# q turned by VectorE instead of TensorE, and v loaded by two heads, from the third batch on, in a threshold attention with a SoLU feed-forward layer

## The chip, the cores and the metric

The kernel runs on one core of a Trainium2 chip. The metric is the device time of one execution in microseconds; each kernel is run several times and the median is given. A profile is of one execution, and its span, from the first to the last instruction, is slightly shorter than the device time of that execution.

## The reference

Inputs are float32: q, k and v of 8 batches, 8 heads, 576 rows and 64 columns, and the weights of a feed-forward layer (w_in and w_out arrive as float64, 512 KB for 128x512). Cut to what matters:

```python
scores = scale * np.matmul(q, k.transpose(0, 1, 3, 2))          # scale = 1/8
thresh = np.max(scores, axis=-1, keepdims=True) - tau
scores = np.where(scores >= thresh, scores, -1000000000.0)
attn = softmax(scores)
x = np.matmul(attn, v)           # then (B,H,S,D) -> (B*S, H*D): 4608 x 512
h = x @ w_in                     # 4608 x 1024
solu = h * softmax(h)
ln = (solu - mean) / sqrt(var + 1e-06) * g_ln
out = ln @ w_out                 # 4608 x 512
```

The softmax is over all 576 keys of a row; the order in which keys are summed and queries are computed is free, as long as q's rows, k's rows, v's rows and the output's rows are matched.

## The kernel before

**Tiling.** Heads are taken in pairs: pair i holds heads 2hp and 2hp+1 of batch b, with i = 4b + hp, so there are 32 pairs. A pair's q and k are needed with the 64 columns of each head on the partitions (`qT`, `kT`: 128 partitions, two heads). The 576 queries of a pair are worked on as two kinds of 256 queries each (kind 0 and 1) and a rest of 64 (kind 2, which takes the rests of all four pairs of a batch together, from `qe`). A slot is 128 queries of two heads against 576 keys; a batch has 18 slots (PER), the program has 144 (NS).

**Rounds.** The program is one hand-written order of all engines' instructions (`tc.manual_schedule`): a loop over rounds `rnd`, one slot of scores each, in which every engine gets its share. In a round TensorE computes the scores of the slot (L460, into the PSUM tiles s0 and s1, which have one buffer each), then a quarter of the feed-forward work: half of the first product (`ff_h`, L625) or half of the second (`ff_o`, L729), so that two h rounds and two o rounds follow one another. In h rounds it also does one product with v (`attend_steps`, L569), due three or more rounds after the slot. VectorE takes the row maxima (`maxes`, L482), ScalarE the ramp and the exponential (`ramp` L497, `exps` L506), GpSimd the normalising in the next round (L513 to L516), VectorE then transposes the weights in 32x32 blocks (`blocks`, L528), and three or four DMAs move them into `wT` (L537 to L544). The feed-forward steps (L640 to L717) are spread over the rounds by the lists `middle` and `late`, and `ff_out` and `ff_store` copy and store the output.

**q and k.** For batches 0 and 1, TensorE transposes q and k with an identity (`turn`, L324) into spare columns of s0 and s1, ahead of the scores of a round, and ScalarE and VectorE copy the results out (`q_item`: L360 and L364; `e_item` for the last 64 rows: L404 and L408; `k_item`: L385). The list `preps` says in which round an item may go. From batch 2 on, k is treated in another way: `load_natural` loads it with four DMAs of 32 partitions per pair, in an order of keys (i, a, t) with 9 keys in a run, `turn_natural` transposes it on VectorE in 32x32 blocks (L192) into `flip`, and two DMAs write it to `kT` (L195). q still goes through `preps`: four turns and one for the rest, for each pair. The dictionaries `load_at` and `turn_at` give the rounds.

**v.** For b > 1, `load_v` loads four heads into a tile of 128 partitions: both halves of the partitions hold all four heads, since the weights of two groups of queries lie on the two halves. It uses four DMAs, each of two heads to 64 partitions.

**Queues.** All loads, moves and stores in the steady part are issued by SP, in program order. A DMA that waits for an engine holds up those behind it. In a round SP gets, in this order: the swap of V (L707), the moves to wT, the stores (L756), the writes of a turned k (L195), then the loads.

**Buffers.** The tiles q, k and ends have two buffers, v three, qT six, kT and qe seven, flip one. They decide from which round on a load can start.

Of the kernel before, what the change touches and what calls it, by code (L numbers as in the profile page):

```python
# [8 lines left out]
F32 = mybir.dt.float32  # L9
# [11 lines left out]
def kernel(  # L21
# [128 lines left out]
    def load_v(b, hf, parts=(0, 1, 2)):  # L150
        d = halves.setdefault((b, hf), {})
        hs = slice(4 * hf, 4 * hf + 4)

        if b > 1:
            if 0 in parts:
                d["v"] = loads.tile([P, 4, NK, D], F32, tag="v", bufs=3, name="v")
            for part in parts:
                two, u = divmod(part, 2)
                nc.sync.dma_start(
                    out=d["v"][ROWS[u], 2 * two : 2 * two + 2].rearrange("p h m d -> p h (m d)"),  # L160
                    in_=v[b, hs][2 * two : 2 * two + 2].rearrange("h (p m) d -> p h (m d)", m=NK),
                )
            return
        if 0 in parts:
            d["v"] = loads.tile([P, 4, NK, D], F32, tag="v", bufs=3, name="v")
        rest = v[b, hs, 0:SM, :].rearrange("h (p t) d -> p h (t d)", t=4)
        for part, to, rows, of in (
            (0, 0, slice(0, P), slice(0, P)), (1, 4, ROWS[0], ROWS[1]), (1, 4, ROWS[1], ROWS[0])
        ):
            if part in parts:  # L170
                nc.sync.dma_start(
                    out=d["v"][rows, :, to : to + 4].rearrange("p h t d -> p h (t d)"),
                    in_=rest[of],
                )
        for rows in ROWS if 2 in parts else ():
            nc.sync.dma_start(
                out=d["v"][rows, :, NK - 1], in_=v[b, hs, SM:S, :].rearrange("h p d -> p h d")
            )

    def load_natural(i):  # L180
        b, hp = divmod(i, NP)
        src = k[b, 2 * hp : 2 * hp + 2].rearrange("h (i a t) d -> a h i (t d)", a=2, t=NK)
        raw = loads.tile([P, 4, 4, D], F32, tag="k", name="k")
        natural[i] = raw = raw.rearrange("p h t d -> p (h t d)")[:, 0 : NK * D]
        for g in range(4):
            a, h = divmod(g, 2)
            nc.sync.dma_start(out=raw[32 * g : 32 * g + 32], in_=src[a, h])

    def turn_natural(i):
        raw = natural.pop(i)  # L190
        flip = loads.tile([P, 2, NK, 32], F32, tag="flip", bufs=1, name="flip")
        nc.vector.transpose(out=flip, in_=raw.rearrange("p (t x g) -> p g t x", g=2, x=32))  # L192
        to = pair(i)["kT"]
        for a in range(2):
            nc.sync.dma_start(  # L195
                out=to[:, 32 * NK * a : 32 * NK * (a + 1)],
                in_=flip[ROWS[a]].rearrange("p g t x -> p g (t x)"),
            )
# [119 lines left out]
    def turn(spare, x, lhsT_of, rows=2, swap=False):  # L318

        o = spare["base"] + 64 * x  # L320
        to = slice(o, o + 64)
        for r in range(rows):
            for y in range(2):
                nc.tensor.matmul(  # L324
                    out=spare[r][ROWS[y], to], lhsT=lhsT_of(r, y),
                    rhs=swapped[ROWS[1]] if swap and r else ident[ROWS[r], ROWS[r]],
                    start=True, stop=True,
                )
# [9 lines left out]
    def pair(i):  # L338
        if i not in pairs:
            pairs[i] = dict(  # L340
                qT=heads.tile([P, SM], F32, tag="qT", bufs=6, name="qT"),
                kT=heads.tile([P, S], F32, tag="kT", name="kT"),
                qe=heads.tile([P, ST], F32, tag="qe", name="qe"),
            )
        return pairs[i]
# [46 lines left out]
    def e_item(i):  # L392
        src, h0 = source(i)
        last = k_parts(i)[:, NK - 1] if i < 2 * NP else None

        def make(spare, x):
            turn(
                spare, x, lambda r, y: ends[i // NP][ROWS[r], 2 * (i % NP) + y],
                2 if i < 2 * NP else 1,
            )  # L400

        def keep(spare, x, r):
# [4 lines left out]
            elif last is not None:  # L407
                (nc.scalar.copy if spare.get("eased") else nc.vector.tensor_copy)(  # L408
                    out=last, in_=seen(spare, 1, x, 1)[:, 0].rearrange("p (k c) -> p c k", c=2)
                )  # L410
# [28 lines left out]
    def scores(s, items):  # L439
# [10 lines left out]
        for ks in (slice(SM, S), slice(0, SM)):  # L450
            for h in range(2):
                for y in range(2):
                    if kind < 2:
                        d = pairs[b * NP + hp]
                        t = P * (2 * kind + r) + 64 * y
# [92 lines left out]
    def attend_steps(key):  # L548
# [7 lines left out]
        for e in range(2) if kind == 2 else [None]:  # L556
            for m in range(NK):
                for u in range(2):
                    d, h0 = source(b * NP + (hp if e is None else e + 2 * u))
                    for h in range(2):  # L560
                        if e is None:
                            to = y[ROWS[h], u, 0:P].rearrange("p (r g x) -> p g r x", r=2, g=2)
                            rhs = wT[ROWS[u], :, m, :, h]
                        else:
# [5 lines left out]
                            out=to, lhsT=d["v"][ROWS[u], h0 + h, m ^ 4 * u if m < 8 and b < 2 else m],  # L570
# [5 lines left out]
    def attended(key):  # L576
        b, kind, hp = key
        tag, y = units.pop(key)["y"]
        y = y.rearrange("p (u n) -> p u n", u=2)[:, :, 0:P].rearrange("p u (r y) -> p u r y", r=2)
# [6 lines left out]
        else:  # L586
# [4 lines left out]
            to = xh[b, kind][:, hp].rearrange("p (r u y) -> p u r y", r=2, u=2)  # L591
# [130 lines left out]
    def ff_o(t, part):  # L722
        d = ffn[t]
        if part == 0:
            d["otag"], d["o"] = take("o_ps")
        for m in range(NC * part, NC * part + NC):
            for r in range(2):
                for z in range(2):
                    nc.tensor.matmul(  # L729
                        out=d["o"][ROWS[z], 512 * r : 512 * r + 256],  # L730
# [16 lines left out]
    def ff_store(t, last):  # L747
        d = ffn.pop(t)
        if len(t) == 1:
            rows = out.rearrange("(b s) m -> s b m", s=S)[SM:S, 2 * t[0] : 2 * t[0] + 2]  # L750
# [25 lines left out]
    for i in range(NP, NPAIR):  # L776
        b, hp = divmod(i, NP)
        if b == 1:
            at = (13, 15, 19, 20)[hp]
        else:  # L780
            at = PER * (b - 1) + ((6, 12, 16, 21) if b == 2 else (6, 9, 12, 17))[hp]
        if b == 1:
            preps += [
                (at, 3, lambda i=i: k_item(i, slice(0, 3)), i),
                (at, 1, lambda i=i: k_item(i, slice(3, 4)), i),
            ]
        preps += [
            (at, 1, lambda i=i: e_item(i), i),
# [4 lines left out]
    turn_at = {}  # L793
# [11 lines left out]
    for i in range(2 * NP, NPAIR):  # L805
        b, hp = divmod(i, NP)
        if b == 2:
            at = (24, 30, 34, 39)[hp]
        else:
            at = PER * b + 4 * hp - (11 if b % 2 else 13)  # L810
        turn_at[at] = i
        load_at.setdefault(at - 3, []).append(lambda i=i: load_natural(i))
        if hp % 2:
            load_at.setdefault(PER * (b - 1) + (9 if hp == 3 else -1), []).append(
                lambda b=b, hf=hp // 2: load_one(b, hf, "q")
            )
            at, by = (PER * b + 4, 1) if hp == 3 else (PER * b - 9, 2)
            for part in range(4):
                load_at.setdefault(at + by * part, []).append(
                    lambda b=b, hf=hp // 2, part=part: load_v(b, hf, (part,))  # L820
                )

    with tc.manual_schedule():
# [29 lines left out]
        while True:  # L853
# [88 lines left out]
            elif step == ("h", 1):  # L942
# [9 lines left out]
                late.setdefault(at, []).append(lambda t=cur, at=at: ff_turn(t, at))  # L952
# [27 lines left out]
            for job in late.pop(rnd, []):  # L980
                job()
            if rnd in turn_at:
                turn_natural(turn_at[rnd])
# [48 lines left out]
```

## Time and profile before

| | before |
|---|---|
| runs | 879.71 us median of 3 (874.94 to 881.91) |
| profiled execution | 880.11 us, span 878.3 us |
| mean granted TensorE clock | 0.979 (0.82 and 0.84 in the first 109 us, then 1.00) |
| L324, TensorE transposes | 1440 records, 35.23 us busy |
| L360, q copied by ScalarE | 480 ns for 128x256 |
| L364, q copied by VectorE | 479 ns for 128x256, 26 from s_ps |
| L404, rest of q copied by ScalarE | 313 ns for 128x64, 28 from s_ps |
| L192, k transposed by VectorE | 24 of 732 ns |
| L516, weights scaled by GpSimd | 288 of 770 ns |
| SP issues: k, 72 KB | 96, 4.1 us to landing |
| SP issues: q, 512 KB | 15, 5.1 us to landing |
| SP issues: v, 288 KB | 48, 4.8 us to landing |
| SP issues: kT from flip, 144 KB | 48, 2.6 us to landing |
| SP issues: wT, 288 KB | 160, 6.5 us to landing |
| DMA moved | 161.59 MB, the ring that SP uses busy 72.6% of 16 engines' span |

The page gives for each engine the time in which it was busy, its share of the span and the number of its instructions (PE is TensorE, PEld its weight loads, DVE VectorE, ACT ScalarE, POOL GpSimd). Under it stand rows of 40 digits: the busy share of each fortieth of the span, in tenths. A line in order of time has the start, the duration, the engine, the line of the code, the operation, what it writes and reads, how many were merged, and in brackets the idle time of the engine ahead of it with what ended it. A TensorE matmul of float32 leaves two records; the ends of matmuls are modelled, and records overlap in time since four 64x64 tiles of the array work at once.

### The profile page before, as it was taken

Reading aid. Unit: us, or ns where it says so; the run is one execution under the profiler, and the core shown is the slowest. Engines: PE = TensorE matmul, PEld = TensorE weight load, DVE = VectorE, ACT = ScalarE, POOL = GpSimd, SP = SyncE. Lnnn points to the kernel's source line nnn. Section 1 sums busy time; section 2 is a strip of 40 time slices with the busy share of each in tenths; the row PEclk is TensorE's granted clock in tenths of the full one; section 3 lists DMA queues with packets and bytes.
Section 4 is the critical chain, followed back from the end, with each engine's and each line's share of the span. In section 5 each row is a group of like instructions: output and inputs, shape, how many; then the busy total and the mean of one; then the engine's idle time right before and its main releaser. Section 6 shows DMA issues by size and latency. Waiting matters only on the chain. (4 is left out here: it accounts for less than half of the span.)

```text
span 878.3 us, 37901 instructions
## 1 busy us (share of the span) xinstructions
PE 831.3 (95%) x16225; PEld 585.2 (67%) x16225; DVE 680.0 (77%) x1248; ACT 586.8 (67%) x1201; POOL 471.0 (54%) x890
## 2 busy tenths in 40 slices
PE   4677899999999999999999999999999999999997
PEld 3353676866677777777776766777677677777655
DVE  5998787888788888888788888888778887877351
ACT  5977776777767777777667667777676776775121
POOL 2877655555555555555555555555455555555120
PEclk9878899999999999999999999999999999999999
DMA  7999877887877777887778786887678776765322
GB/s 231 276 255 256 203 189 190 209 220 175 197 190 205 193 184 186 214 201 168 175 179 215 185 200 169 196 218 185 159 182 221 179 178 152 177 140 139 66 49 49
DMA packets 84008, 161.59 MB, mean 184 GB/s; under 512 B 18808, under 2 KB 48512, under 8 KB 83840
## 3 DMA queue, kind: packets, MB, share of 16 engines
q1 hardware_dynamic: 82704, 157.17, 72.6%
q8 instruction: 127, 2.08, 1.1%
q10 hardware_dynamic: 1136, 2.00, 0.7%
q14 instruction: 41, 0.34, 0.1%
HBM read 46.14 MB, written 9.44 MB: 63 GB/s over the span
## 5 line engine op out<-in xcount | busy, mean ns | idle before, releaser
L482 DVE CUSTOM_DVE_ANT_0 w<-s_ps,tau_t 128x576 f32<-128x576 f32 x280 | 200.7, 754 | 123.4 <-PE s_ps L460 92.5
L497 ACT ACTIVATE w<-s_ps,nth 128x576 f32<-128x576 f32 x280 | 200.1, 743 | 107.5 <-DVE nth L482 101.3
L729 PE MATMUL o_ps<-w,uT 64*64 64x256 f32 x4608 | 264.5, 376 | 2.1 <-DVE uT L717 1.1
L729 PEld LDWEIGHTS o_ps<-w,uT 64*64 64x64 f32 x4608 | 218.8, 133 | 59.9 <-issue 16.8
L516 POOL TENSOR_SCALAR w<-w,sm 128x576 f32<-128x576 f32 x288 | 218.4, 770 | 14.3
L506 ACT ACTIVATE w<-w,ntau 128x576 f32<-128x576 f32 x288 | 220.2, 771 | 0.0
L625 PE MATMUL h_ps<-w,xh 64*64 64x512 f32 x1856 | 217.3, 592 | 0.0
L528 DVE STREAM_TRANSPOSE T<-w 128x576 f32<-128x576 f32 x288 | 206.2, 751 | 7.7 <-POOL w L516 7.4
L569 PEld LDWEIGHTS pv<-wT,v 64*64 64x64 f32 x5760 | 164.0, 136 | 50.5 <-issue 39.5
L460 PE MATMUL s_ps<-kT,qT 64*64 64x64 f32 (+1 forms) x2048 | 166.9, 423 | 16.6 <-ACT w L497 13.3
L569 PE MATMUL pv<-wT,v 64*64 64x128 f32 (+1 forms) x5760 | 167.5, 263 | 6.8 <-DMA wT<-T 3.5
L513 POOL TENSOR_SCALAR sm<-sm 128x2 f32<-128x2 f32 x144 | 36.5, 254 | 234.3 <-ACT w L506 231.2
L625 PEld LDWEIGHTS h_ps<-w,xh 64*64 64x64 f32 x1856 | 94.3, 134 | 98.4 <-issue 95.5
L514 POOL TENSOR_TENSOR sm<-sm,mone 128x2 f32<-128x2 f32 x144 | 104.3, 724 | 12.0
L691 ACT ACTIVATE V<-u,nb,rs 128x1024 f32<-128x1024 f32 x36 | 44.7, 1241 | 52.6 <-POOL nb L681 52.6
L460 PEld LDWEIGHTS s_ps<-kT,qT 64*64 64x64 f32 x2048 | 60.4, 139 | 24.8 <-ACT w L497 18.8
L592 ACT COPY xh<-pv 128x256 f32<-128x256 f32 x64 | 23.7, 370 | 61.4 <-PE pv L569 61.4
L506 ACT ACTIVATION_READ_ACCUMULATOR w<-w,ntau 128x1 f32 x288 | 56.7, 197 | 0.0
L696 DVE TENSOR_SCALAR u<-u,rs,nb 128x1024 f32<-128x1024 f32 x36 | 42.3, 1176 | 12.6 <-ACT V L691 12.4
L655 DVE TENSOR_TENSOR u<-h_ps,u 128x1024 f32<-128x1024 f32 x36 | 42.8, 1190 | 11.3 <-ACT u L649 11.3
L717 DVE STREAM_TRANSPOSE uT<-V 128x1024 f32<-128x1024 f32 x36 | 43.8, 1218 | 9.1 <-DMA V<-u 9.0
L640 DVE TENSOR_REDUCE hm<-h_ps 128x1 f32<-128x1024 f32 x36 | 43.0, 1193 | 9.8 <-PE h_ps L615 5.6
(87 smaller groups left out, 620.6 us busy)
## 6 DMA issues: line engine op xcount, KB each, us to landing
wT<-T SPq DMA_DIRECT2D x160, 288.0 KB, 6.5
wT<-T SPq DMA_DIRECT2D x64, 576.0 KB, 5.4
v<-in_v_dram SPq DMA_DIRECT2D x48, 288.0 KB, 4.8
V<-u SPq DMA_DIRECT2D x144, 64.0 KB, 3.4
out_dram<-ob SPq DMA_DIRECT2D x71, 128.0 KB, 2.7
q<-in_q_dram SPq DMA_DIRECT2D x15, 512.0 KB, 5.1
k<-in_k_dram SPq DMA_DIRECT2D x96, 72.0 KB, 4.1
kT<-flip SPq DMA_DIRECT2D x48, 144.0 KB, 2.6
```

The costliest lines, as they stand in the source:

```text
L460: nc.tensor.matmul(out=ps[h][ROWS[y], ks], lhsT=lhsT, rhs=d["kT"][ROWS[h], ks], start=True, stop=True,)
L482: nc.vector.tensor_tensor_reduce(out=w, in0=ps[:, 0:S], in1=(zero if loose else tau_t).to_broadcast([P, S]), scale=1.0, scalar=BIG, op0=AL ...
L497: nc.scalar.activation(out=d["w"][x], in_=d["w"][x] if d["loose"] else d["ps"][x][:, 0:S], func=AF.Prelu, bias=d["nth"][x], scale=-1.0, al ...
L506: nc.scalar.activation(out=w, in_=w, func=AF.Exp, bias=ntau, scale=1.0, accum_out=sm[:, x : x + 1])
L514: nc.gpsimd.tensor_tensor(out=sm, in0=sm, in1=mone, op=ALU.pow)
L516: nc.gpsimd.tensor_scalar(out=w, in0=w, scalar1=sm[:, x : x + 1], scalar2=1.0, op0=ALU.mult, op1=ALU.mult)
L528: nc.vector.transpose(out=T[:, :, r, h, :], in_=w)
L569: nc.tensor.matmul(out=to, lhsT=d["v"][ROWS[u], h0 + h, m ^ 4 * u if m < 8 and b < 2 else m], rhs=rhs, start=m == 0, stop=m == NK - 1,)
L625: mm = nc.tensor.matmul(out=h[ROWS[y], f], lhsT=x[ROWS[r], c, ROWS[y]], rhs=w1_parts[ROWS[r], c, part ^ r], start=part == 0 and c == 0, st ...
L691: nc.scalar.activation(out=V, in_=u, func=AF.Identity, bias=nb, scale=rs)
L717: nc.vector.transpose(out=uT, in_=d["V"].rearrange("p y (m x) -> p m y x", x=32))
L729: nc.tensor.matmul(out=d["o"][ROWS[z], 512 * r : 512 * r + 256], lhsT=d["uT"][ROWS[r], m].rearrange("p y x -> p (y x)"), rhs=w2[ROWS[r], m ...
```

## The change

It concerns batches 2 to 7, with a small shift in one feed-forward tile of batch 0.

- q is loaded like k, and both by four heads: `load_natural(i, nm, a)` makes one DMA of 128 partitions (4 heads x 32), 288 KB, for pairs i and i+1; a is the half of the rows. There are four such loads for two pairs, two of q and two of k.
- GpSimd multiplies q by the scale in place (`scale_natural`), one round ahead of the turn.
- `turn_natural(i, nm, a)` transposes 128x576 on VectorE and writes the two halves of the partitions to the two pairs' qT or kT with one DMA each. `flip` now takes the buffers of `ends`, which are two.
- `gather_ends` takes the last 64 queries (every ninth row) out of `qT` into `qe` on GpSimd. qT has 576 columns for these batches.
- `preps` holds batch 1 only; TensorE no longer turns q of later batches, and the copies of it are gone.
- v is loaded with four DMAs of another cut: heads 0 to 3 into slots 0 and 2 of all 128 partitions (576 KB), heads 1 and 2 into slot 1 of 128 partitions (288 KB), and two of one head to 64 partitions (144 KB each). On the upper half of the partitions head n now lies in slot n-1.
- The queries of a slot are other ones, since q's rows are ordered (a, t, i): the scores' lhsT, the layout of the product's output, its copy to xh, the bank of half of the o tiles and the rows of the stores follow this order.
- The transpose `ff_turn` of the tile (0, 1, 1) moves from the end of a round to the middle of a round two later.

The diff, cut:

```diff
         if b > 1:
             if 0 in parts:
                 d["v"] = loads.tile([P, 4, NK, D], F32, tag="v", bufs=3, name="v")
+            to = d["v"].rearrange("p h m d -> p h (m d)")
+            rows = v_rows[64 * (H * b + 4 * hf) :][0:256]
             for part in parts:
-                two, u = divmod(part, 2)
-                nc.sync.dma_start(
-                    out=d["v"][ROWS[u], 2 * two : 2 * two + 2].rearrange("p h m d -> p h (m d)"),
-                    in_=v[b, hs][2 * two : 2 * two + 2].rearrange("h (p m) d -> p h (m d)", m=NK),
-                )
+                nc.sync.dma_start(**(
+                    dict(
+                        out=to.rearrange("p (e o) n -> p o e n", o=2)[:, 0],
+                        in_=rows.rearrange("(e r) n -> r e n", e=2),
+                    ),
+                    dict(out=to[:, 1], in_=rows[64:192]),
+                    dict(out=to[ROWS[1], 3], in_=rows[0:64]),
+                    dict(out=to[ROWS[0], 3], in_=rows[192:256]),
...
             )
 
-    def load_natural(i):
-        b, hp = divmod(i, NP)
-        src = k[b, 2 * hp : 2 * hp + 2].rearrange("h (i a t) d -> a h i (t d)", a=2, t=NK)
-        raw = loads.tile([P, 4, 4, D], F32, tag="k", name="k")
-        natural[i] = raw = raw.rearrange("p h t d -> p (h t d)")[:, 0 : NK * D]
-        for g in range(4):
-            a, h = divmod(g, 2)
-            nc.sync.dma_start(out=raw[32 * g : 32 * g + 32], in_=src[a, h])
-
-    def turn_natural(i):
-        raw = natural.pop(i)
-        flip = loads.tile([P, 2, NK, 32], F32, tag="flip", bufs=1, name="flip")
+    qk_rows = {
+        nm: x.rearrange("b h (i a t) d -> a (b h i) (t d)", a=2, t=NK)
+        for nm, x in (("q", q), ("k", k))
+    }
+    v_rows = v.rearrange("b h (p m) d -> (b h p) (m d)", m=NK)
+
+    def load_natural(i, nm, a):
+        raw = loads.tile([P, 4, 4, D], F32, tag=nm, name=nm)
+        natural[i, nm, a] = raw = raw.rearrange("p h t d -> p (h t d)")[:, 0 : NK * D]
+        nc.sync.dma_start(out=raw, in_=qk_rows[nm][a, 64 * i : 64 * i + P])
+
+    def scale_natural(i, a):
+        raw = natural[i, "q", a]
+        nc.gpsimd.tensor_scalar(
+            out=raw, in0=raw, scalar1=scl, scalar2=1.0, op0=ALU.mult, op1=ALU.mult
+        )
+
+    def gather_ends(i):
+        d = pair(i)
+        nc.gpsimd.tensor_copy(
+            out=d["qe"].rearrange("p (x a) -> p a x", a=2),
+            in_=d["qT"].rearrange("p (a t x) -> p a t x", a=2, x=32)[:, :, NK - 1],
+        )
+
+    def turn_natural(i, nm, a):
+        raw = natural.pop((i, nm, a))
+        flip = loads.tile([P, 2, NK, 32], F32, tag="ends", name="flip")
         nc.vector.transpose(out=flip, in_=raw.rearrange("p (t x g) -> p g t x", g=2, x=32))
-        to = pair(i)["kT"]
-        for a in range(2):
+        for j in range(2):
             nc.sync.dma_start(
-                out=to[:, 32 * NK * a : 32 * NK * (a + 1)],
-                in_=flip[ROWS[a]].rearrange("p g t x -> p g (t x)"),
+                out=pair(i + j)[nm + "T"][:, 32 * NK * a : 32 * NK * (a + 1)],
+                in_=flip[ROWS[j]].rearrange("p g t x -> p g (t x)"),
             )
 
...
         if i not in pairs:
+            qT = heads.tile([P, S], F32, tag="qT", bufs=6, name="qT")
             pairs[i] = dict(
-                qT=heads.tile([P, SM], F32, tag="qT", bufs=6, name="qT"),
+                qT=qT[:, 0:SM] if i < 2 * NP else qT,
                 kT=heads.tile([P, S], F32, tag="kT", name="kT"),
                 qe=heads.tile([P, ST], F32, tag="qe", name="qe"),
...
                         d = pairs[b * NP + hp]
-                        t = P * (2 * kind + r) + 64 * y
+                        t = P * (2 * kind + r) if b < 2 else 32 * NK * r + P * kind
+                        t += 64 * y
                         lhsT = d["qT"][ROWS[h], t : t + 64]
                     else:
...
                         if e is None:
-                            to = y[ROWS[h], u, 0:P].rearrange("p (r g x) -> p g r x", r=2, g=2)
+                            how = "p (r g x) -> p g r x" if b < 2 else "p (g r x) -> p g r x"
+                            to = y[ROWS[h], u, 0:P].rearrange(how, r=2, g=2)
                             rhs = wT[ROWS[u], :, m, :, h]
...
                         nc.tensor.matmul(
-                            out=to, lhsT=d["v"][ROWS[u], h0 + h, m ^ 4 * u if m < 8 and b < 2 else m],
+                            out=to,
+                            lhsT=d["v"][
+                                ROWS[u], (h0 + h - u) % 4 if b > 1 else h0 + h,
+                                m ^ 4 * u if m < 8 and b < 2 else m,
+                            ],
                             rhs=rhs,
                             start=m == 0, stop=m == NK - 1,
...
-            to = xh[b, kind][:, hp].rearrange("p (r u y) -> p u r y", r=2, u=2)
+            how = "p (r u y) -> p u r y" if b < 2 else "p (u g x r) -> p u g r x"
+            to = xh[b, kind][:, hp].rearrange(how, u=2, r=2, **({} if b < 2 else {"g": 2}))
...
         d = ffn[t]
+        other = len(t) == 3 and t[0] > 1 and t[2]
         if part == 0:
             d["otag"], d["o"] = take("o_ps")
         for m in range(NC * part, NC * part + NC):
             for r in range(2):
                 for z in range(2):
                     nc.tensor.matmul(
-                        out=d["o"][ROWS[z], 512 * r : 512 * r + 256],
+                        out=d["o"][ROWS[z], 512 * (r ^ other) : 512 * (r ^ other) + 256],
                         lhsT=d["uT"][ROWS[r], m].rearrange("p y x -> p (y x)"),
...
+        elif t[0] > 1:
+            b, kind, m = t
+            rows = out[b * S : b * S + S, :].rearrange("(k t) m -> k t m", t=NK)
+            rows = rows[:, 4 * kind + 2 * m : 4 * kind + 2 * m + 2]
...
     preps = []
-    for i in range(NP, NPAIR):
-        b, hp = divmod(i, NP)
-        if b == 1:
-            at = (13, 15, 19, 20)[hp]
-        else:
-            at = PER * (b - 1) + ((6, 12, 16, 21) if b == 2 else (6, 9, 12, 17))[hp]
-        if b == 1:
-            preps += [
-                (at, 3, lambda i=i: k_item(i, slice(0, 3)), i),
-                (at, 1, lambda i=i: k_item(i, slice(3, 4)), i),
-            ]
+    for i in range(NP, 2 * NP):
+        at = (13, 15, 19, 20)[i - NP]
         preps += [
+            (at, 3, lambda i=i: k_item(i, slice(0, 3)), i),
+            (at, 1, lambda i=i: k_item(i, slice(3, 4)), i),
             (at, 1, lambda i=i: e_item(i), i),
             (at, 4, lambda i=i: q_item(i), i),
         ]
...
-    for i in range(2 * NP, NPAIR):
-        b, hp = divmod(i, NP)
+    for i in range(2 * NP, NPAIR, 2):
+        b, hf = divmod(i // 2, 2)
+        ats = ((-5, -3), (-1, 1)) if hf else ((-13, -11), (-9, -7))
         if b == 2:
-            at = (24, 30, 34, 39)[hp]
-        else:
-            at = PER * b + 4 * hp - (11 if b % 2 else 13)
-        turn_at[at] = i
-        load_at.setdefault(at - 3, []).append(lambda i=i: load_natural(i))
-        if hp % 2:
-            load_at.setdefault(PER * (b - 1) + (9 if hp == 3 else -1), []).append(
-                lambda b=b, hf=hp // 2: load_one(b, hf, "q")
-            )
-            at, by = (PER * b + 4, 1) if hp == 3 else (PER * b - 9, 2)
-            for part in range(4):
-                load_at.setdefault(at + by * part, []).append(
-                    lambda b=b, hf=hp // 2, part=part: load_v(b, hf, (part,))
-                )
+            ats = ((-3, -2), (-1, 1)) if hf else ((-13, -11), (-9, -5))
+        for nm, pieces_at in zip("qk", ats):
+            for a, at in enumerate(pieces_at):
+                at += PER * b
+                load_at.setdefault(at - 3, []).append(
+                    lambda i=i, nm=nm, a=a: load_natural(i, nm, a)
+                )
+                turn_at[at] = i, nm, a
+                if nm == "q":
+                    scale_at[at - 1] = i, a
+        for j in range(2):
+            ends_at[PER * b + ats[0][1] + 4 + j] = i + j
+        for part, at in enumerate((4, 5, 5, 7) if hf else (-9, -7, -5, -3)):
+            load_at.setdefault(PER * b + at, []).append(
+                lambda b=b, hf=hf, part=part: load_v(b, hf, (part,))
+            )
...
-                late.setdefault(at, []).append(lambda t=cur, at=at: ff_turn(t, at))
+                if cur == (0, 1, 1):
+                    middle.setdefault(rnd + 6, []).append(lambda t=cur, at=rnd + 6: ff_turn(t, at))
+                else:
+                    late.setdefault(at, []).append(lambda t=cur, at=at: ff_turn(t, at))
...
+            if rnd in scale_at:
+                scale_natural(*scale_at[rnd])
+            if rnd in ends_at:
+                gather_ends(ends_at[rnd])
             if rnd in turn_at:
-                turn_natural(turn_at[rnd])
+                turn_natural(*turn_at[rnd])
```

## The prediction

> **What bounds the kernel now.** I read the page first, then the groups of instructions with shapes kept apart, then the order of time of TensorE and VectorE in one stretch of the middle.
>
> From the page, the busy times and two of the rows of slices:
>
> ```profile
> PE 831.3 (95%) x16225; PEld 585.2 (67%) x16225; DVE 680.0 (77%) x1248; ACT 586.8 (67%) x1201; POOL 471.0 (54%) x890
> ...
> PE   4677899999999999999999999999999999999997
> DVE  5998787888788888888788888888778887877351
> ```
>
> TensorE is at nine tenths from the sixth slice on. In the stretch from 283 to 743 us it is busy 457.17 of 460.00 us at a full granted clock. So there the time is the length of its instruction stream, unless another engine falls behind it. The chain of waits covers only the last per cent and says nothing about this stage; I leave it aside.
>
> TensorE in order of time, around one transposed pair (36 records) and through one cycle:
>
> ```profile
> 400.57 0.22 PE L324 MATMUL s_ps<-ident,ends 64*64 64x64 f32 x2
> ...
> 401.10 1.19 PE L460 MATMUL s_ps<-kT,qe 64*64 64x64 f32 x15
> 402.07 3.65 PE L625 MATMUL h_ps<-w,xh 64*64 64x512 f32 x32
> 405.51 2.19 PE L569 MATMUL pv<-wT,v 64*64 64x128 f32 x72
> 407.47 1.19 PE L460 MATMUL s_ps<-kT,qT 64*64 64x64 f32 x16
> ...
> 413.85 1.20 PE L460 MATMUL s_ps<-kT,qT 64*64 64x64 f32 x16
> 414.82 3.67 PE L729 MATMUL o_ps<-w,uT 64*64 64x256 f32 x64
> 418.27 1.20 PE L460 MATMUL s_ps<-kT,qT 64*64 64x64 f32 x16
> ...
> 422.70 1.20 PE L460 MATMUL s_ps<-kT,qT 64*64 64x64 f32 x16
> ```
>
> A round runs from one group of scores (L460) to the next. The cycle is two h rounds of 6.37 and 6.38 us (scores, first feed-forward product, product with v) and two o rounds of 4.42 and 4.43 us (scores, second product). No idle time is noted between these lines. A round with a pair of q turned is longer: from 396.09 to 401.10 is 5.01 instead of 4.43 us.
>
> VectorE in the two o rounds of that cycle:
>
> ```profile
> 416.54 1.43 DVE L528 STREAM_TRANSPOSE T<-w 128x576 f32<-128x576 f32 x2
> 417.90 1.19 DVE L655 TENSOR_TENSOR u<-h_ps,u 128x1024 f32<-128x1024 f32 x1
> 419.51 0.76 DVE L482 CUSTOM_DVE_ANT_0 w<-s_ps,tau_t 128x576 f32<-128x576 f32 x1 [0.43 <-PE s_ps L460]
> ...
> 424.04 0.76 DVE L482 CUSTOM_DVE_ANT_0 w<-s_ps,tau_t 128x576 f32<-128x576 f32 x1 [0.34 <-PE s_ps L460]
> ```
>
> In an o round VectorE has 0.43 and 0.34 us to spare, against 1.23 and 1.44 us after h rounds. That is where added VectorE work can hurt.
>
> [...]
>
> **The parts.** NPAIR is 32; the change concerns the 24 pairs of batches 2 to 7.
>
> *TensorE, removed.* Per pair 4 + 32 records (e and q items). From the first L324 to L460 is 401.10 - 400.57 = 0.53 us; from the round lengths 5.01 - 4.43 = 0.58. I take 0.57: 24 x 0.57 = 13.7 us. Bounds 12.7 and 14. All of it is on TensorE's stream, which sets the end, so all counts.
>
> *Stalls that go with it.* Around 173 to 181 us, where batch 1 ends and TensorE has little to fill in, it waited for the turned q:
>
> ```profile
> 173.46 0.33 PE L324 MATMUL s_ps<-ident,ends 64*64 64x64 f32 x4 [0.19 <-DVE both L482]
> 174.13 0.27 PE L324 MATMUL s_ps<-swapped,q 64*64 64x64 f32 x2 [0.23 <-DVE both L482]
> 180.15 0.33 PE L460 MATMUL s_ps<-kT,qT 64*64 64x64 f32 x4 [0.93 <-ACT qT L360]
> 180.79 1.19 PE L460 MATMUL s_ps<-kT,qT 64*64 64x64 f32 x12 [0.30 <-ACT w L497]
> ```
>
> These sum to 1.65 us. I take 1.3 as gone, from 0 to 2.5, since the turn of feed-forward tile (0, 1, 1), 1.2 us of VectorE, also leaves this stretch for round 31, whose second product is not before round 32. The score slots themselves still wait there for VectorE and ScalarE.
>
> *ScalarE.* Minus 24 x (0.48 L360 + 0.31 L404) = 19 us; it was not the bound, so nothing on the path. The copy of the product with v (L592, 370 ns, 64 of them, 48 changed) now writes every second element. It ends at 414.51 and the o matmuls start at 414.82, so 0.3 us are free. [...] I take 0.
>
> *VectorE.* Plus 24 transposes x 0.73 (row of L192) = 17.5, minus 24 x 0.48 (L364) = 11.5: plus 6 us. The turns now stand on odd rounds; from batch 3 on half of all 48 fall in the first o round. There 0.73 against 0.43 us of slack leaves VectorE 0.30 us late. In the next round ScalarE's last ramp (L497) ends at 421.80 and TensorE's scores come at 422.70, so 0.9 us covers 0.30; the second o round's 0.34 then pays it back. Cost 0. If that cover were gone, 0.30 a time. The wait that the turn adds (for q's load and its scaling) has behind it on VectorE the next row maxima, and behind these ScalarE and the scores.
>
> *GpSimd.* Plus 24 scalings x 0.77 (L516, same operation and shape) and 24 gathers of 128x64, not shown before: between the 0.21 us of the 64x32 copy at L207 and 0.77; I take 0.25. That is 24 us on 471, while L513 waited 231 us for ScalarE. The worst place is the second o round: normalising 2.5, statistics 1.7, scaling 0.8, gather 0.25 is 5.2 us in 4.43, so the next normalising starts up to about 1 us late. VectorE's transposes of it come in the first h round, behind L482 and L696, and TensorE needs them three rounds on. I take 0, bound 0.3 x 12 = 4 us.
>
> *Queue of SP.* Out: 96 k, 12 q, 6 end and 48 v issues. In: 48 loads, 48 more writes of flip to qT, 48 v issues. 210 become 192 with k and q turned counted, at about 0.6 us each: 11 us less. Each turn's two writes wait for VectorE on SP, with v, wT and V behind them; the row of 48 kT<-flip had such waits of 1.2 us and less. A q load issued at the end of its round must land before GpSimd scales it two rounds later, at least 8.8 us; landing was 5.1 us (q), 4.1 (k). Cost 0.
>
> *DMA bytes.* q is now also moved once inside SBUF, 48 x 144 KB, 7 MB on 161.6; rows from HBM grow from 1 KB and 256 B to 2304 B. PV waited for wT or other DMAs 0.7 us in 283 to 743, with wT landing in 4.7 to 8.4 us. One v load is twice as large (576 KB). I take 0.5 us of new waits, from -0.5 to 5.
>
> *Nothing:* the new order of q's rows, of PV's output, of o's halves (XOR with other) and of the stores moves addresses, not counts; a store still has 1 KB rows. The matmul shapes stay, so L460, L569, L625 and L729 cost the same.
>
> **Sum** against the profiled execution (span 878.3, 880.1 with what lies around it, 0.4 above the median of the runs shown): 880.1 - 13.7 - 1.3 + 0.5 = 865.6; against the median 865.2. I say **865**.
>
> **Rivals.**
> 1. *VectorE becomes the bound in o rounds.* For it: 0.73 exceeds 0.43. Against: the 0.9 us of PSUM slack. If each of the 24 turns there costs TensorE 0.30: 865 + 7 = 872.
> 2. *The added DMA traffic delays wT.* 144 KB at 184 GB/s is 0.8 us; 24 products late by that: 865 + 19 = 884, hardly a loss. For it, DMA engines at 77%; against it, the 0.7 us. A third of that is likelier, 871.
> 3. *Slower: q's load arrives after GpSimd wants it.* GpSimd waits in order, normalising and then VectorE wait behind it, and the row maxima stall TensorE. The margin is 8.8 - 5.1 = 3.7 us plus about 1.2 of VectorE's slack; from a landing of 10 us on it costs what exceeds that. To give back 15 us and 9 more it needs 1 us in each of 24 scalings, so landings of 11 us: 890. The longest q landing after 130 us was 7.3.
> 4. *The change does less than it says:* if only VectorE's second half of q were replaced, L324 would still be there and nothing moves: 879. The diff takes all e and q items of batches 2 to 7 away, so hardly.
>
> **Chances.** Forecast 0.74; rival 1 0.10, rival 2 0.09 (mostly at 871, a third of it at 880 or above), rival 3 0.04, rival 4 0.03. Only a change by over 1% (8.8 us) can be told from none here. Faster by over 1% is all below 871: most of the forecast and of rivals 1 and 2, 0.87. Within 1%: 0.08. Slower: 0.05. Range: 13.7 may be 14, 2.5 of stalls may go, and runs spread by 3.5 us, which gives 859 below; rivals 1 and 2 set 873 above.
>
> **What would show it.** L324 falls from 1440 records to 576; the rounds that were 5.0 and 6.96 us are 4.43 and 6.37; L192's successor counts 48; GpSimd gains 24 lines of 0.77; VectorE's 0.43 us before L482 in o rounds goes to 0 while TensorE notes no gap. It is wrong if L460 gets waits for ScalarE's ramps in o rounds (rival 1), L569 for wT (rival 2), or GpSimd's scaling for q's load (rival 3).

## The result, and the profile after

| | before | after |
|---|---|---|
| runs | 880.68 us, median of 22 | 875.36 us, median of 22 |
| ratio of after to before | | 0.9938, 95% interval 0.9919 to 0.9957 |
| profiled execution | 880.11 us, span 878.3 | 876.26 us, span 874.4 |

The change takes 5.3 us, a third of the 15 that were forecast. The page of the changed kernel, its busy times and the two rows of slices:

```profile
PE 822.0 (94%) x15361; PEld 599.8 (69%) x15361; DVE 682.6 (78%) x1248; ACT 573.1 (66%) x1153; POOL 499.4 (57%) x938
...
PE   5667999999999999999999999999899999999997
DVE  5998787888788887888788887888778887787351
```

TensorE has 864 fewer matmul records, 9 us less busy time, and is no longer as full: in the stretch from 279 to 738 us it is busy 452.07 of 459.00 us, where it had 457.17 of 460.00. So the stream of matmuls became shorter and got gaps. The list of waits of the changed kernel (engine and what it wanted, what ended the wait: us in all, times, longest) says who waits now:

```profile
DVE uT L746 <- DMA V<-u: 37.5, 23, 4.0
POOL q L199 <- DMA q<-in_q_dram: 29.0, 13, 5.2
DVE T L547 <- POOL w L535: 21.1, 20, 2.6
```

The same list of the kernel before has for the first of these:

```profile
DVE uT L717 <- DMA V<-u: 9.0, 7, 4.1
```

VectorE waits four times as long for the swap of V between partitions, and GpSimd, in whose order the normalising stands, waits for q's loads.

Where the time went is read best by rounds. I took the length of each round from the starts of its scores (L460, in the changed kernel L479). From round 43 to round 143 the stage took 555.59 us before and 552.71 after, in one trace each:

| rounds | after minus before |
|---|---|
| 19 rounds in which TensorE turned a pair of q | -10.9 us, 0.57 each |
| 56, 75 and 76, 92, 111 and 112, 128: product with v of the last 64 queries of a batch (rest rounds) | +3.7 |
| 61, 69, 77, 97, 101, 109, 133: first o rounds | +4.2 |
| all others | +0.1 |

From round 23 to 43, where the other five pairs were turned, it is 105.1 and 104.1 us: rounds 29 to 31, where the stalls were, fell from 17.04 to 15.76 us, but round 34 came to 8.25 instead of 6.38.

A first o round that got longer, number 61, in the changed kernel, VectorE in order of time (start and duration in us, line and operation, in square brackets the wait before it):

```profile
340.51 0.75 DVE L501 CUSTOM_DVE_ANT_0 w<-s_ps,tau_t 128x576 f32<-128x576 f32 x1
...
345.57 1.25 DVE L746 STREAM_TRANSPOSE uT<-V 128x1024 f32<-128x1024 f32 x1 [2.95 <-DMA V<-u]
```

TensorE's order of time in the same round:

```profile
345.01 1.24 PE L479 MATMUL s_ps<-kT,qT 64*64 64x64 f32 x15
346.96 3.69 PE L759 MATMUL o_ps<-w,uT 64*64 64x256 f32 x64 [0.71 <-DVE uT L746]
```

VectorE stands 2.95 us at the transpose of V; TensorE then finds uT not ready for the second product, which begins 1.95 us after the scores' start. In the kernel before it began 0.97 us after them (413.85 and 414.82 in the prediction's lines). That is the whole difference: the round is 5.43 us instead of 4.43.

### The profile page after: what moved, and what is told of

Its sections match the earlier page's. It is cut to its first block, busy times and chain, and to the rows that moved or that the text cites. A ratio compares the mean times of both kernels' runs of the same rounds, so it can differ in the third digit from the quotient of the medians.

```text
span 874.4 us, 36148 instructions
## 1 busy us (share of the span) xinstructions
PE 822.0 (94%) x15361; PEld 599.8 (69%) x15361; DVE 682.6 (78%) x1248; ACT 573.1 (66%) x1153; POOL 499.4 (57%) x938
## 5 line engine op out<-in xcount | busy, mean ns | idle before, releaser
L759 PE MATMUL o_ps<-w,uT 64*64 64x256 f32 x4608 | 269.2, 376 | 5.1 <-DVE uT L746 3.1
L759 PEld LDWEIGHTS o_ps<-w,uT 64*64 64x64 f32 x4608 | 214.8, 133 | 68.5 <-issue 17.1
L516 ACT ACTIVATE w<-s_ps,nth 128x576 f32<-128x576 f32 x280 | 196.7, 740 | 92.4 <-DVE nth L501 84.8
L501 DVE CUSTOM_DVE_ANT_0 w<-s_ps,tau_t 128x576 f32<-128x576 f32 x280 | 199.5, 748 | 64.1 <-PE s_ps L479 56.0
L535 POOL TENSOR_SCALAR w<-w,sm 128x576 f32<-128x576 f32 x288 | 221.3, 780 | 14.3
L547 DVE STREAM_TRANSPOSE T<-w 128x576 f32<-128x576 f32 x288 | 207.7, 755 | 23.7 <-POOL w L535 21.1
L654 PE MATMUL h_ps<-w,xh 64*64 64x512 f32 x1856 | 222.5, 592 | 0.0
L589 PEld LDWEIGHTS pv<-wT,v 64*64 64x64 f32 x5760 | 173.6, 136 | 50.1 <-issue 28.1
L589 PE MATMUL pv<-wT,v 64*64 64x128 f32 (+1 forms) x5760 | 176.3, 264 | 13.0 <-DMA wT<-T 5.3
L479 PE MATMUL s_ps<-kT,qT 64*64 64x64 f32 (+1 forms) x2048 | 173.5, 419 | 13.1 <-ACT w L516 11.8
L654 PEld LDWEIGHTS h_ps<-w,xh 64*64 64x64 f32 x1856 | 111.3, 134 | 82.7 <-issue 59.3
L479 PEld LDWEIGHTS s_ps<-kT,qT 64*64 64x64 f32 x2048 | 70.2, 139 | 21.9 <-ACT w L516 17.5
L746 DVE STREAM_TRANSPOSE uT<-V 128x1024 f32<-128x1024 f32 x36 | 44.4, 1234 | 37.5 <-DMA V<-u 37.5
L678 ACT ACTIVATE u<-h_ps,hm 128x1024 f32<-128x1024 f32 x36 | 40.2, 1115 | 31.4 <-DVE hm L669 21.7
L725 DVE TENSOR_SCALAR u<-u,rs,nb 128x1024 f32<-128x1024 f32 x36 | 36.5, 1014 | 22.2 <-ACT V L720 22.2
L684 DVE TENSOR_TENSOR u<-h_ps,u 128x1024 f32<-128x1024 f32 x36 | 42.8, 1189 | 10.9 <-ACT u L678 10.9
```

The costliest lines, as they stand in the source:

```text
L479: nc.tensor.matmul(out=ps[h][ROWS[y], ks], lhsT=lhsT, rhs=d["kT"][ROWS[h], ks], start=True, stop=True,)
L501: nc.vector.tensor_tensor_reduce(out=w, in0=ps[:, 0:S], in1=(zero if loose else tau_t).to_broadcast([P, S]), scale=1.0, scalar=BIG, op0=AL ...
L516: nc.scalar.activation(out=d["w"][x], in_=d["w"][x] if d["loose"] else d["ps"][x][:, 0:S], func=AF.Prelu, bias=d["nth"][x], scale=-1.0, al ...
L535: nc.gpsimd.tensor_scalar(out=w, in0=w, scalar1=sm[:, x : x + 1], scalar2=1.0, op0=ALU.mult, op1=ALU.mult)
L547: nc.vector.transpose(out=T[:, :, r, h, :], in_=w)
L589: nc.tensor.matmul(out=to, lhsT=d["v"][ROWS[u], (h0 + h - u) % 4 if b > 1 else h0 + h, m ^ 4 * u if m < 8 and b < 2 else m,], rhs=rhs, sta ...
```

## The experiments

Twelve runs were made in three groups, each group on one chip beside runs of the kernel before; a ratio is always to the kernel before of the same group.

**The saving alone.** q of batches 2 to 7 is left out. The edit, cut:

```diff
-    for i in range(NP, NPAIR):
+    for i in range(NP, 2 * NP):
         b, hp = divmod(i, NP)
...
+                pairs[i] = dict(
+                    qT=q_fix, kT=heads.tile([P, S], F32, tag="kT", name="kT"), qe=qe_fix
+                )
```

> The kernel before, with q of batches 2 to 7 left out: their scores use one fixed tile for qT and qe, so TensorE's turns of q and the copies of them are gone and nothing takes their place (q is still loaded). It measures the first two terms of the sum alone. Theory A (the saving of 13.7 us on TensorE and 1.3 us of stalls was rightly sized, and the changed kernel gives it back elsewhere): 880.7 - 15 = 866, 864 to 868. Rival B (the turns' records overlapped with other work and a round without them is hardly shorter): 873 to 877, like the changed kernel.

869.37 us, ratio 0.9898 (0.9873 to 0.9923): 9 us, between the two. In rounds 43 to 143 the turned pairs' time is gone in full (10.8 us), but the rest rounds of the table above have grown by 2.7, without any added work. Round 56 in this kernel, TensorE in order of time:

```profile
314.57 1.16 PE L468 MATMUL s_ps<-kT,q_fix 64*64 64x64 f32 x16
315.54 1.90 PE L633 MATMUL h_ps<-w,xh 64*64 64x512 f32 x16
317.26 0.28 PE L577 MATMUL pv<-wT,v 64*64 64x64 f32 x4
317.95 0.86 PE L577 MATMUL pv<-wT,v 64*64 64x64 f32 x42 [0.41 <-DMA wT<-T]
```

and in the kernel before:

```profile
319.56 1.94 PE L625 MATMUL h_ps<-w,xh 64*64 64x512 f32 x16
321.28 0.91 PE L569 MATMUL pv<-wT,v 64*64 64x64 f32 x47
```

In a rest round the product with v is woven into the round's share of the first feed-forward product and begins after half of it (16 of 32 records), 1.7 us after that share's start; elsewhere it begins after all of it. Here TensorE now arrives ahead of wT and waits. Rounds 54 to 56 together took 17.89 us before and 17.95 here: the pair turned in round 54 had filled time in which TensorE would have waited for wT. Rounds 90 to 92 are 17.94 and 18.05. The other part of the growth, 1.3 us, lies in rounds 111 and 112, and 1.0 of it is a gap of TensorE for which the profile names no cause; more of it below.

In rounds 23 to 43 this kernel took 103.88 us against 105.14. Five turned pairs and the stalls lie there, 4.1 us by the prediction's figures, and 1.3 came. But the run does not measure the second term as the change has it: it leaves the transpose of tile (0, 1, 1) in its place, and the prediction counted on its move. Rounds 29 to 31 took 17.02 us here and 15.76 in the changed kernel. At the head of round 31 TensorE now waits for ScalarE's ramp, where it waited 0.93 us for the copy of q and 0.30 for the ramp:

```profile
178.50 0.33 PE L468 MATMUL s_ps<-kT,qT 64*64 64x64 f32 x4 [1.29 <-ACT w L505]
179.17 1.19 PE L468 MATMUL s_ps<-kT,qT 64*64 64x64 f32 x12 [0.35 <-ACT w L505]
```

**GpSimd's scaling left out.** Edit: the loop no longer calls `scale_natural`.

> The changed kernel without GpSimd's scaling of q in batches 2 to 7 (q is used unscaled there). Theory A (GpSimd waits in order for q's loads, 29 us in 13 waits, which delays normalising and the statistics in rounds 34 and 39 to 41; SP's order delays the swap of V as well): the waits of GpSimd vanish and some 3 us with them, 872. Rival C (the whole loss comes from GpSimd): 866. Rival D (only the order on SP counts): 875, no change.

872.22 us, ratio 0.9929 (0.9901 to 0.9957), against 0.9938 of the changed kernel: not to be told apart from it, and too wide to separate A from D. C is out. The trace shows that GpSimd's waits are gone and round 34 is back at 6.38 us, while VectorE's waits for V stayed (41.9 us) and rounds 61 and 97 as well (5.79 and 5.93). So the late q loads explain round 34, and not the o rounds. (Round 34 was 6.84 to 8.25 us in four traces of the changed kernel and of the one with moved loads below.)

**Loads behind the swaps of V.** One number. Loads that stood in second o rounds, right ahead of a swap, go to first o rounds; those of second h rounds go to first h rounds, behind a swap:

```diff
-                load_at.setdefault(at - 3, []).append(
+                load_at.setdefault(at - (3 if b == 2 else 4), []).append(
```

> The changed kernel with the loads of q and k from batch 3 on issued one round earlier, so on odd rounds, behind the four swaps of V in SP's order and not ahead of them. Theory D (V's swap issued 1.2 us later than before, because a load stands ahead of it on SP, is what makes VectorE wait 37.5 us for V): these waits fall to under 20 us, the o rounds 69, 77, 101 and 109 are 4.43 us again, and rounds 61, 97 and 133, which also have a load of v ahead, partly: 872 to 873. Rival E (the added bytes in the DMA rings make V land later, whatever the order): 875, waits as before.

871.00 us, ratio 0.9916 (0.9896 to 0.9937). The stage from round 43 to 143 fell from 552.71 to 548.16 us in its trace, and VectorE's waits for V from 37.5 to 24.7 us, not to under 20. It was run again beside the changed kernel on one chip:

> The changed kernel as it is, on the same chip as the three that follow, so that they can be compared with it. 0.994 of the kernel before.

> The changed kernel with the loads of q and k from batch 3 on one round earlier, behind the swaps of V. Theory D (SP's order): 4 to 5 us faster than the changed kernel on the same chip, 0.989 of the kernel before, as its trace showed. Rival (the first run's gain was chance, the order matters by 2 us at most): 0.992.

After: 875.96 us, 0.9948 (0.9928 to 0.9968). With the loads moved: 871.91 us, 0.9893 (0.9866 to 0.9921). The intervals do not touch; the difference is 0.55%, 4.8 us. SP's queue in the changed kernel (first trace), rounds 59 and 60, which start at 332.26 and 338.63 (the time is that of issuing):

```profile
333.27 0.57 SPq L556 DMA_DIRECT2D wT<-T  x1
333.89 2.92 SPq L558 DMA_DIRECT2D wT<-T  x2
336.86 0.98 SPq L160 DMA_DIRECT2D v<-in_v_dram  x1
337.94 0.95 SPq L195 DMA_DIRECT2D q<-in_q_dram  x1
338.99 2.48 SPq L736 DMA_DIRECT2D V<-u  x4
```

and with the loads moved, the same rounds, which start at 330.35 and 336.72:

```profile
331.36 0.57 SPq L556 DMA_DIRECT2D wT<-T  x1
331.98 2.87 SPq L558 DMA_DIRECT2D wT<-T  x2
334.90 1.03 SPq L160 DMA_DIRECT2D v<-in_v_dram  x1
336.03 2.64 SPq L736 DMA_DIRECT2D V<-u  x4
```

SP is still issuing the moves of one round, until 336.81 us, when VectorE has already finished V of the next, at 336.08, and the q load, which belongs to the round before, stands between. It is not urgent, and it delays four small transfers of 64 KB that are: the first is issued 2.91 us after V is finished. Over the 25 tiles from round 40 to 143, nothing stood between the moves to wT and the swap 19 times before and 5 times in the changed kernel, where a load of k (10 times) or of q (9) did; with the loads moved it is 22 times. The median time from the end of the second half of V (L725) to the first issue of a swap was 0.44 us before, 1.80 in the changed kernel, and 0.81 with the loads moved. VectorE's waits for V in the two traces of this group, the changed kernel and the one with moved loads:

```profile
DVE uT L746 <- DMA V<-u: 42.8, 24, 4.0
DVE uT L746 <- DMA V<-u: 21.9, 20, 4.0
```

So the order counts, and bytes alone (theory E) are out; before, these waits were 9.0 us. The edit does two more things. GpSimd's waits for q fall from 25.8 to 4.2 us, since the loads are earlier; but the run without scaling had none of these waits and kept 3.3 of the 4.2 us in first o rounds. And the loads change their place among the other transfers too: from round 43 to 143 the trace is 5.2 us shorter, of which 2.0 lie in the first o rounds of the table, 1.8 in the rest rounds, and 1.5 elsewhere. Between the first traces of the two kernels it is 3.1 and 2.2 us, of which 1.5 are the gap in round 111 described below, and 0.7 lost elsewhere. The swap of V accounts for the first part; how the rest came about was not separated.

**v cut as before.** The edit, cut; the index of v's heads in the product goes with it, and the third late load goes back to its old round, one later:

```diff
+                two, u = divmod(part, 2)
+                nc.sync.dma_start(
+                    out=d["v"][ROWS[u], 2 * two : 2 * two + 2].rearrange("p h m d -> p h (m d)"),
+                    in_=v[b, hs][2 * two : 2 * two + 2].rearrange("h (p m) d -> p h (m d)", m=NK),
+                )
```

> The changed kernel with v loaded as before, by four DMAs of two heads to 64 partitions, at the old rounds. Theory F (the load of 576 KB in rounds 58, 94 and 130 stands ahead of V's swap and costs about 1 us in each of rounds 61, 97, 133): 873. Rival G (the other cut of v is a gain, with wider transfers): slower than the changed kernel, 877.

879.22 us, ratio 0.9990 (0.9970 to 1.0010): theory F falls and G holds. In the changed kernel the new cut of v is worth 0.5%. Most of it lies in round 34 of this profile, 11.22 us against 8.25, where GpSimd waits up to 6.9 us for q. Loads of one size, from issue to landing (the last figure), on 128 partitions in the changed kernel and on 64 here:

```profile
v<-in_v_dram SPq DMA_DIRECT2D x12, 288.0 KB, 4.2
v<-in_v_dram SPq DMA_DIRECT2D x48, 288.0 KB, 5.2
```

**Earlier loads, then a later product.** Two steps on top of the moved loads: q's loads so early that GpSimd scales in second h rounds only (for batch 2, the second pair of them in rounds 26 and 27), and the odd batches' first late v load one round earlier; then the product with v in rest rounds begins after three quarters of the round's share of the first feed-forward product (24 of 32 records in the trace) and not after half of it. The expectations below call these a half and a quarter:

```diff
-            for _, _ in zip(range(24 * (c > 0)), beside):
+            for _, _ in zip(range(36 * (c > 1)), beside):
```

> As the one above, and also: q's loads still earlier, so that GpSimd scales q only in second h rounds and never waits for a load; batch 2's second q loads in rounds 26 and 27; the first v load of the second half one round earlier in odd batches, not ahead of V's swap. Theory (waits of GpSimd for q and what is left of the late swap cost some 2 us): GpSimd's waits for q go to near 0, rounds 34, 97 and 133 to 6.37, 4.43 and 4.43 us: 0.986 to 0.987 of the kernel before. Rival (what is left sits in the rounds with the rest of the queries, 39, 56, 75, 92, 111, 128): 0.989, as above.

> As the one above, and in rounds 39, 56, 75, 92, 111 and 128 the product with v starts after half of the first feed-forward product, not after a quarter. Theory H (in these rounds TensorE waits for wT or for a PSUM tile whatever was saved before, 6 us in all, which is where the missing part of the saving of 15 us went): 3 to 5 us faster than the one above, 0.981 to 0.983. Rival (the wait only moves to the end of the round): no change, 0.987.

869.84 us, 0.9868 (0.9836 to 0.9901), and 867.73 us, 0.9841 (0.9813 to 0.9869). The first step does not stand out from the moved loads (0.9893), nor the second from the first; together they do from the changed kernel, and 867.73 us is the fastest version in which nothing is left out. In the trace of the first, GpSimd's waits for q's loads are gone and rounds 34, 97 and 133 are 6.37, 4.45 and 4.43 us as expected, but rounds 84 to 86 took 1.7 us more, with a wait for wT. In the trace of the second, rest rounds 56, 75, 92, 111 and 128 sum to 1.6 us above the plain 6.37 each, against 7.2 in the first. Of these 7.2, 1.44 us are a gap of TensorE in round 111 that the profile puts down to nothing but its own issuing; the second has one of 0.97 us in round 93.

**Is the missing saving hidden in the rest rounds?** The later product alone, the turns alone, and both:

> The kernel before without the turns of q of batches 2 to 7 (q of these batches left out, one fixed tile in its place), again, beside the two that follow: 0.990 of the kernel before.

> The kernel before, with the product with v in rounds 39, 56, 75, 92, 111 and 128 started after half of the first feed-forward product. Its trace shows 3 us above the plain lengths in these rounds. Theory H (they wait for a result that is late whatever TensorE saves ahead of it): 2 to 3 us faster than before, 0.997. Rival: no change, 1.000.

> Both: no turns of q in batches 2 to 7 (that q left out), and the product with v later in these six rounds. Theory H (the missing part of the saving was hidden in these rounds): 5 to 6 us faster than without turns alone, 0.984, so that the turns cost 13 us measured against the kernel above. Rival (the turns cost 10 us wherever these products stand): 0.987.

| | product as before | product later |
|---|---|---|
| q turned by TensorE | 1 | 1.001 (0.999 to 1.003), 880.90 us |
| no turns | 0.9876 (0.985 to 0.9902), 871.15 us | 0.9828 (0.9796 to 0.9859), 864.88 us |

Moving the product gains nothing in the kernel before, where the expected 2 to 3 us did not come. Once the turns are gone the point estimate gains 0.48%, though these two intervals touch. Taking the turns away is worth 0.9828 / 1.001 = 0.982, 16 us, with the later product, and 11 (9 in the first run) without. Hiding in the rest rounds would give that. But the traces show a rival. Of the 4.3 us that the rest rounds of the first table lose from the kernel without turns to the one with both edits, 3.5 lie in round 111, which has this in the former and no such gap in the latter:

```profile
625.81 0.70 PE L577 MATMUL pv<-wT,v 64*64 64x64 f32 x33 [2.38 <-issue]
```

The profile names no release for this gap. One of 1.35 to 2.60 us stands in round 111 or 112 of eight of the fourteen traces, and of the two traces of the kernel with moved loads one has it (1.57 us) and one has not. With the later product alone it is 2.60 us, against 1.35 in the kernel before. Without it the rest rounds lose 0.2 us by the later product in the kernel before and 1.9 once the turns are gone. So hiding in the rest rounds is seen, in rounds 56 and 92 above, but its share of the 5 us between 16 and 11 is not shown; the cause of the gap stays open.

**v once more,** in the fastest version:

> The version with early loads and the later product, but v by four DMAs of two heads to 64 partitions as in the kernel before. In the changed kernel this cut cost 0.5%, most of it in round 34, where GpSimd waited for q. Theory (the cut mattered through that late load alone): as the version itself, 0.984 to 0.985. Rival (loads to 64 partitions hold up the DMA rings everywhere): 0.989.

870.89 us, 0.9881 (0.9848 to 0.9914), between the two and overlapping with the version's own 0.9841: unclear. Its trace has TensorE waiting for wT in rounds 100 and 120 (8.25 and 8.38 us where 6.37 is plain), which speaks for the rival; but the version itself has 7.15 us in round 100. Loads of v of 288 KB landed in 5.0 us here and 4.2 in the version itself. What this is worth outside round 34 stays open.

## Why the prediction was wrong

**TensorE, removed: the time of a pair was right, "so all counts" failed.** Each turned round became 0.57 us shorter, as read. But without the turns and with nothing added, only 9 to 11 of the 15 us reached the end. By the traces of the two such runs, some 3 us of the 10.8 that the 19 pairs from round 43 on gave were lost in rest rounds: waits for wT, and the gap without a named cause. TensorE was nearly full, yet some of what it was full with stood where it would otherwise have waited. The 2.83 us that it was not busy in the prediction's stretch were a sign: the trace of before has 1.28 us of them in rest rounds 75 and 111, for ScalarE's copy of an output tile, and 1.35 in the gap of round 112.

**Stalls: about half.** In these two runs they became waits of 1.29 and 2.13 us for ScalarE's ramp. In the changed kernel, with the tile's transpose moved, rounds 29 to 31 lost 1.28 us, of which 0.57 are a turned pair's: 0.7 of the 1.3.

**Queue of SP: this step failed.** It counted issues (18 fewer, 11 us less at 0.6 us each; the loads shown above take 0.95 and 0.98) and set the cost at 0. What counted was where a load stands in the order: moving the loads away from the swaps of V, and a round earlier, gave 4.8 us. The prediction named V as queued behind the turn's writes, but not behind the loads, and looked at the waits of the kernel before instead of at SP's order in the kernel after.

**"Two rounds later, at least 8.8 us" failed too.** It took the load as issued in its own round. SP runs late, so the q load of round 58 above is issued at 337.94, towards the end of the h round after it. It landed 6.46 us later, and GpSimd, which wanted it 3.2 us after the issue, waited 3.3. There were 13 such waits, 29 us. This is rival 3's mechanism, though at a price of some 2 us in round 34 of the trace and none that the run without scaling could resolve.

**VectorE: right.** The changed kernel in a cycle of o rounds that start at 411.33 and 415.76, the next at 420.19:

```profile
414.09 1.43 DVE L547 STREAM_TRANSPOSE T<-w 128x576 f32<-128x576 f32 x2
415.45 1.18 DVE L684 TENSOR_TENSOR u<-h_ps,u 128x1024 f32<-128x1024 f32 x1
416.56 0.76 DVE L213 STREAM_TRANSPOSE flip<-k 128x576 f32<-128x576 f32 x1
417.24 0.72 DVE L501 CUSTOM_DVE_ANT_0 w<-s_ps,tau_t 128x576 f32<-128x576 f32 x1
```

The idle time ahead of L501 is gone, and both rounds are 4.43 us. Rival 1 did not come: from round 43 on TensorE notes no wait for a ramp in this trace.

**GpSimd: sizes right.** The groups of the changed kernel:

```profile
L199 POOL TENSOR_SCALAR q<-q,scl 128x576 f32<-128x576 f32 x24 | 17.9, 746 | 31.1 <-DMA q<-in_q_dram 29.0 <-DMA wT<-T 2.1
L205 POOL COPY qe<-qT 128x64 f32<-128x64 f32 x24 | 6.3, 264 | 0.0
L621 ACT COPY xh<-pv 128x256 f32<-128x256 f32 x64 | 24.9, 389 | 63.7 <-PE pv L589 63.7
```

0.75 and 0.26 us against 0.77 and 0.25. VectorE's waits for the weights that GpSimd normalises rose from 7.4 to 21.1 us; the run without scaling had 10.3 and was not measurably faster. The last row is ScalarE's copy of the product with v, 389 ns on average against 370. The 48 copies that now write every second element took 398, against 372 before. The prediction took 0 for this step, an estimate: no row of before has a copy at it. Here it costs 26 ns a copy, so it is nearly free and not wholly.

**DMA bytes: the sign of v was wrong.** The new cut and q's move inside SBUF were priced together at 0.5 us of loss; the new cut is a gain of some 4 us. The run with the old cut shows the sign, and its loads of 288 KB to 64 partitions landed in 5.2 us, against 4.2 for those to 128 in the changed kernel; by what mechanism was not shown. The 0.7 us that the prediction gives for wT or other DMAs are idle time of weight loads and belong to other DMAs: no product waits for wT in that stretch of the kernel before, where wT landed in 4.2 to 8.4 us. Over the whole trace the product's waits for wT rose from 3.5 to 5.3 us, so little of rival 2 came.

The parts, in points of a per cent: turns gone -1.0 to -1.2 (without the tile's move), v -0.5, place of the loads +0.55. What remains to the measured -0.6 is about +0.4, with an error of about 0.4. It would be the other additions, and no run assigns it.

## What to carry to other kernels

When work is taken off the bounding engine, look at each place where that engine next needs a result of another: what it saves ahead of such a place may only be a longer wait there; here 9 to 11 of 15 us reached the end. When DMAs are added to a queue, don't count issues; write down the new order, take the queue as late as the trace shows it, and ask which urgent transfer a lazy one now precedes. Here the place of the loads, one round apart, made 4.8 us, a third of the gain that was forecast.

## What the runs showed of the hardware

VectorE's normalising of half a feed-forward tile took 1176 ns on average in the kernel before. The source views, minimum, median and maximum in ns, of the kernel before:

```profile
L696 DVE TENSOR_SCALAR u<-u,rs,nb x36: 810/1190/1298, 95.5 to 860.2; 128x1024 f32<-128x1024 f32 x36
```

The same of the changed kernel:

```profile
L725 DVE TENSOR_SCALAR u<-u,rs,nb x36: 801/862/1861, 94.7 to 856.2; 128x1024 f32<-128x1024 f32 x36
```

It took 0.81 us alone, and 1.19 to 1.30 when GpSimd's scaling of the weights is running or starts with it: after 100 us, all 30 such instances of before lie beside an L516 and end 0.55 us after it, and the 5 short ones lie beside nothing. In the changed kernel, where GpSimd is late, 19 of 35 are short; 15 of the other 16 end 0.55 us after an L535, the same scaling, and four of the short ones overlap with an L535 all the same. So the instruction is 0.4 to 0.5 us longer beside most of these scalings; why was not shown. The prediction has no term for it, and no run here measured what it is worth in the kernel's time.
